# Transition to the experts laid out anew, and a 512-wide final product

## The chip, the cores and the metric

One core of one Trainium2 chip. The metric is the device time of one execution in microseconds; the time before is the median of three runs, 1478.5 (1477.45 to 1479.95). The five compute queues are PE (matrix products), ACT, DVE, POOL, and SP, which here only issues DMAs. A second row of PE in the profile, PEld, is its weight loads.

## The reference

The input x is 8 x 3072 x 256. Three parts follow one another:

```
X = rfft(x, axis=1)                                  # per batch, along the 3072 tokens
Yr = Xr @ w_r - Xi @ w_i + b_r ;  Yi = Xr @ w_i + Xi @ w_r + b_i
y = irfft(softthreshold(Yr) + 1j * softthreshold(Yi))

logits = y @ phi                                     # all 24576 tokens, 32 slots
d = softmax over tokens ; slot_in = d.T @ y          # 32 x 256
slot_out[e] = relu(slot_in[e] @ w1[e]) @ w2[e]       # 8 experts, 4 slots each, 1024 wide
z = (softmax over slots of logits) @ slot_out

h = z @ w_in                                         # 1024 wide
u = h * softmax(h) ; ln = (u - mean) / sqrt(var + 1e-6) * g_ln
out = ln @ w_out                                     # 256 wide
```

The softmax over tokens needs all batches before the first expert can start; the last part needs the experts before its first token. w_in and w_out arrive as 64-bit words and are turned into 32-bit floats on the chip.

## The kernel before

**Phase 1 (0 to about 600 us)** goes over 8 batches of 12 tiles: the Fourier transform as matrix products, the mixing weights, the inverse, the logits, and a running softmax over tokens whose weighted sums (`acc`) are formed in the spectrum (`slots`). The order is written out by hand: `after(lag, fn)` puts a step on a heap, to be issued `lag` ticks later, and the table `LAG` holds the lags. Every engine executes its own list in that order; a wait of one instruction holds up everything behind it on the same engine.

**The decoding** of w_in and w_out lies in phase 1. `decode` (L623 to L646) reads one of eight pieces (128 x 512 words of 64 bits, tile `raw`) with an SP DMA (L634), eight DVE operations, one per tile step, turn it into floats in the tiles `da`, `db`, `dm`, and `dec_out` writes `da` to `win_dram` or `wout_dram` (L660). The next piece's read is issued right behind that write.

**The transition (about 600 to 658 us).** When phase 1's memory is given back, SP issues the read of g_ln (tile `gl`) and of the decoded w_out (`wo`, 1 MB), then of the experts' weights: `wt` (15 of 512 KB), `ws` (11 of 256 KB). POOL scales `wo` by `gl` (L136). Meanwhile the last batch's softmax runs through a chain of small steps: `fwd2` (spectrum of the token weights, `dh`), `sums4` (L604) and `sums` for the running denominator, then `slots`. `gmean` forms the column mean of `wo` and subtracts it (POOL, L600). `csoft`, `csoft2`, `csoft3`, `c_x`, `c_out` make the last batch's softmax over slots and write it to `c_dram`. Behind that come 11 more `ws`, then w_in (`wi`, 1 MB), then the first read of `c_dram` (`ct`). The experts are `ph` (slots times w1), `h1` (relu: ACT L847, DVE L848), transposes, `po` (times w2), `so`; `psl` and `sot` put the slot outputs into place, and `pg` is slot outputs times w_in in four f32 products. So `gst` holds the 32 slots' rows of h, and the last part never forms z.

**Phase 2 (658 us to the end)** takes 192 tiles of 128 tokens. For each tile PE does, in this order, `hmat(i+2)` (two products 512 wide, `hps`), `trans(i)` (eight transposes of u, `pu`), and `prod(i-1)`, the product with w_out. To keep f32 accuracy with the fp32r format, u and w_out are both split into a high and a low part, `uh + ul` and `gw_h + gw_l`, and `prod` adds up three of the four products:

```
for a, w in ((uh, gw_h), (uh, gw_l), (ul, gw_h)):
    for f in range(8):
        mm(ps, a[:, f, :], w[:, f, :], n == 0, n == 23)
```

ACT copies the result (`osb`, L1027), does the exponentials (`expo`), `uh` (L971) and the squares (`vari`); DVE the row maxima (L938), u (L953) and `ul` (L979); POOL scales four tiles at once by the reciprocal standard deviation (L1032) and prepares the pieces of `c`.

Of the kernel before, what the change touches and what calls it, by code (L numbers as in the profile page):

```python
# [33 lines left out]
def kernel(  # L34
# [96 lines left out]

    def load_g():
        SP.dma_start(out=gl, in_=g_ln.rearrange("(k p) -> p k", p=128))
        SP.dma_start(out=wo, in_=wout_dram.rearrange("(k p) d -> p k d", p=128))
        for k in range(8):
            POOL.tensor_scalar(out=wo[:, k, :], in0=wo[:, k, :], scalar1=gl[:, k:k + 1], scalar2=-float(DFF) ** 1.5, op0=ALU.mult, op1=ALU.mult)  # L136


    def phase1(pl: ExitStack, pr_: ExitStack):
# [12 lines left out]
        raw_p = right("raw_p", 1)  # L152
# [339 lines left out]
        def csoft(b):  # L492
# [5 lines left out]
            after(LAG["csoft2"], csoft2, b, c)  # L498

        def csoft2(b, c):  # L500
            ACT.activation(out=c, in_=c, func=AF.Exp)
            after(LAG["csoft3"], csoft3, b, c)

        def csoft3(b, c):
# [36 lines left out]
        def dtr(b, h):  # L541
# [51 lines left out]
        def gmean(z):  # L593
            if z == 0:
                small["pg"] = psg.tile([128, D], F32, name="pgm")
            for k in range(4 * z, 4 * z + 4):
                mm(small["pg"], ones, wo[:, k, :], k == 0, k == 7)
            if z:
                ACT.activation(out=gm[:, 0, :], in_=small["pg"], func=AF.Copy, scale=1.0 / DFF)
                POOL.tensor_tensor(out=wo, in0=wo, in1=gm.to_broadcast([128, 8, D]), op=ALU.subtract)  # L600

        def sums4(b):
            s4 = sm("s4", [1, 4, 32])
            DVE.tensor_scalar(out=s4, in0=small["dh", b][0:1, 0, 0:1, :].to_broadcast([1, 4, 32]), scalar1=float(N), scalar2=None, op0=ALU.mult)  # L604
# [20 lines left out]
        def decode(src, dst):  # L625
            raw = raw_p.tile([128, 512], I64, name="raw", tag="raw")
            a = raw_p.tile([128, 512], I32, name="da", tag="da")
            c = raw_p.tile([128, 512], I32, name="db", tag="db")
            m = raw_p.tile([128, 512], I32, name="dm", tag="dm")
            v = raw.bitcast(I32).rearrange("p (n two) -> p n two", two=2)  # L630
            hi = v[:, :, 1]
            lo = raw.bitcast(U32).rearrange("p (n two) -> p n two", two=2)[:, :, 0]
# [12 lines left out]
                lambda: dec_out(dst, f),  # L645
            ])  # L646

        def dec_step():
            if not dec_ops and decs:
                decode(*decs.pop(0))  # L650
                return
            if dec_ops:
                dec_ops.pop(0)()
                if len(dec_ops) == 1:
                    dec_ops.pop(0)()
                    if decs:
                        decode(*decs.pop(0))
# [133 lines left out]
        load_ws(NS - NT)  # L791
        while heap:
# [3 lines left out]
    def phase2(p2: ExitStack, pw: ExitStack):  # L796
        k_p = p2.enter_context(tc.tile_pool(name="k2_p", bufs=1))
        c_p = p2.enter_context(tc.tile_pool(name="c_p", bufs=2))
        gw_h = k_p.tile([128, 8, D], F32R, name="gw_h")
        gw_l = k_p.tile([128, 8, D], F32R, name="gw_l")  # L800
# [33 lines left out]
        for eh in range(2):  # L834
# [14 lines left out]
            h1s[eh] = h1  # L849
        load_c(0, 1)  # L850
# [12 lines left out]
        DVE.tensor_tensor(out=gw_l, in0=wo, in1=gw_h.bitcast(F32), op=ALU.subtract)  # L863

        for eh in range(2):
# [4 lines left out]
            DVE.tensor_copy(out=so[:, eh, :], in_=po)  # L870
# [327 lines left out]
```

## Time and profile before

| | |
|---|---|
| median of three runs | 1478.5 us (1477.45 to 1479.95) |
| profiled execution | 1476.49 us, its span 1474.7 us |
| PE busy | 1422.3 us, 96% of the span |
| DVE, ACT, POOL busy | 1192.1 us (81%), 1065.2 us (72%), 671.9 us (46%) |

The span runs from the first to the last instruction that the profile holds; the execution's own time is 1.8 us longer. A busy PE is not a PE that is needed: what sets the end is read from the chain of waits, stage by stage.

### The profile page before, as it was taken

The page shows a single profiled execution, that of the slowest core. Times are in us where ns is not written, and L with a number is a line of the kernel's source. Part 1 is how long each engine was busy: PE and PEld are TensorE (multiplying, and loading weights), DVE is VectorE, ACT ScalarE, POOL GpSimd, SP SyncE. Part 2 cuts the span into 40 slices and gives each one's busy share as a digit, 9 for nine tenths or more (in the row PEclk, how much of TensorE's full clock was granted, in tenths as well). Part 3 has the DMA queues.
Part 4 walks back from the last instruction along what each step waited for, and adds up shares of the span by engine and source line. Part 5 has one row for each costly group of instructions (what it writes and reads, how often), then busy time and mean ns, then how long its engine had stood idle before and what let it go on. Part 6 is the DMA issues. An engine that isn't in the chain of part 4 may idle for free.

```text
span 1474.7 us, 31675 instructions
## 1 busy us (share of the span) xinstructions
PE 1422.3 (96%) x12300; PEld 1293.8 (88%) x12300; DVE 1192.1 (81%) x1885; ACT 1065.2 (72%) x2169; POOL 671.9 (46%) x703
## 2 busy tenths in 40 slices
PE   6999999999999999779999999999999999999999
PEld 3888887878788888539999999999999999999998
DVE  6788878887878688548888888888888888888886
ACT  5667565756565655327888888888888888888887
POOL 5556554656465633323344343443434434344343
PEclk8999999999999999898999999999999999999999
DMA  9965554546354540780111111111111111111001
GB/s 268 297 188 147 152 156 128 163 130 181 116 165 117 146 157 30 257 250 30 44 56 46 44 44 44 57 53 50 44 44 58 44 44 44 44 58 45 30 29 44
DMA packets 80102, 149.17 MB, mean 101 GB/s; under 512 B 9104, under 2 KB 45712, under 8 KB 79952
## 3 DMA queue, kind: packets, MB, share of 16 engines
q1 hardware_dynamic: 79952, 147.15, 31.8%
q8 instruction: 96, 1.57, 0.4%
q14 instruction: 54, 0.44, 0.1%
HBM read 91.55 MB, written 55.57 MB: 100 GB/s over the span
## 4 chain that ended last, share of the span: by engine, by line
PE 76%; DVE 11%; DMA 7%; issue 3%; ACT 2%; POOL 1%; SPq 0%; DVEq 0%; ACTq 0%; POOLq 0%
PE po L87 37%; PE pu L90 11%; PE hps L87 6%; PE pb L87 6%; PE s L87 3%; PE pm L87 3%; PE xps L87 3%; PE pa L87 2%; DMA xc<-in_x_dram 2%; DMA ad<-asb 2%; PE sps L90 1%; DVE yb L330 1%; DVE yb L331 1%; DVE xl L289 1%; DVE dm_sb L560 1%
## 5 line engine op out<-in xcount | busy, mean ns | idle before, releaser
L938 DVE TENSOR_REDUCE st<-hps 128x1 f32<-128x1024 f32 x192 | 235.1, 1225 | 121.4 <-PE hps L87 121.4
L979 DVE TENSOR_TENSOR ul<-pu,uh 128x512 fp32r<-128x512 f32 x384 | 246.4, 683 | 0.8 <-ACT uh L971 0.8
L953 DVE SCALAR_TENSOR_TENSOR u<-hps,e 128x1024 f32<-128x1024 f32 x192 | 233.3, 1215 | 2.2 <-ACT e L945 2.1
L334 POOL TENSOR_TENSOR s<-yb,s 128x512 f32<-128x512 f32 x95 | 132.2, 1391 | 223.5 <-DVE s L333 208.5
L87 PE MATMUL po<-gw_h,uh 128*128 128x256 f32 x1536 | 231.1, 293 | 0.0
L988 ACT ACTIVATE sq<-u,st 128x1024 f32<-128x1024 f32 x192 | 224.4, 1169 | 0.0
L945 ACT ACTIVATE e<-hps,st 128x1024 f32<-128x1024 f32 x192 | 213.2, 1110 | 2.9 <-DVE st L938 2.9
L87 PE MATMUL po<-gw_l,uh 128*128 128x256 f32 x1536 | 214.0, 282 | 0.0
L87 PE MATMUL po<-gw_h,ul 128*128 128x256 f32 x1536 | 212.8, 280 | 0.0
L971 ACT ACTIVATE uh<-pu 128x512 fp32r<-128x512 f32 x384 | 208.9, 604 | 3.0 <-PE pu L90 2.9
L90 PEld LDWEIGHTS pu<-ident,u 128*128 128x128 f32 x1536 | 180.7, 141 | 26.0 <-issue 0.4
L90 PE MATMUL pu<-ident,u 128*128 128x128 f32 x1536 | 200.6, 274 | 0.0
L87 PEld LDWEIGHTS po<-gw_h,uh 128*128 128x128 f32 x1536 | 196.5, 191 | 0.0
L87 PEld LDWEIGHTS po<-gw_l,uh 128*128 128x128 f32 x1536 | 196.2, 189 | 0.0
L87 PEld LDWEIGHTS po<-gw_h,ul 128*128 128x128 f32 x1536 | 196.2, 188 | 0.0
L226 POOL TENSOR_TENSOR x<-xc,x 96x512 fp32r<-96x512 f32 x120 | 164.8, 1381 | 41.2 <-ACT x L225 37.4
L1032 POOL TENSOR_TENSOR os<-osb,st 128x1024 f32<-128x1024 f32 x47 | 89.1, 1896 | 180.6 <-issue 172.9
L1027 ACT ACTIVATE osb<-po 128x256 f32<-128x256 f32 x188 | 72.3, 385 | 115.1 <-PE po L87 115.1
L252 ACT ACTIVATE asb<-s 96x512 f32<-96x512 f32 x112 | 66.7, 596 | 82.7 <-PE s L87 72.2
L913 POOL TENSOR_TENSOR c<-ct,c 32x512 fp32r<-32x512 f32 x96 | 123.3, 1285 | 6.7
L1008 POOL TENSOR_TENSOR st<-st 128x4 f32<-128x4 f32 (+1 forms) x51 | 10.2, 200 | 254.7 <-ACT sq L988 254.5
L87 PE MATMUL hps<-gst,c 128*128 128x512 f32 x384 | 120.5, 396 | 5.8 <-DVE u L953 4.3
(189 smaller groups left out, 2628.4 us busy)
## 6 DMA issues: line engine op xcount, KB each, us to landing
apt<-ad SPq DMA_DIRECT2D x96, 256.0 KB, 4.1
out_dram<-os SPq DMA_DIRECT2D x47, 512.0 KB, 2.6
xc<-in_x_dram SPq DMA_DIRECT2D x56, 384.0 KB, 3.9
ad<-asb SPq DMA_DIRECT2D x56, 384.0 KB, 3.5
ct<-c_dram SPq DMA_DIRECT2D x96, 128.0 KB, 2.7
wt<-in_moe_w_dram SPq DMA_DIRECT2D x21, 512.0 KB, 9.5
ws<-in_moe_w_dram SPq DMA_DIRECT2D x22, 256.0 KB, 5.7
xc<-in_x_dram SPq DMA_DIRECT2D x16, 192.0 KB, 5.1
```

The lines of the kernel that those rows point to most:

```text
L87: PE.matmul(out=out, lhsT=lhsT, rhs=rhs, start=start, stop=stop)
L90: PE.transpose(out=out, in_=in_, identity=ident[0:k, 0:k])
L226: POOL.tensor_tensor(out=lo, in0=t, in1=hi.bitcast(F32), op=ALU.subtract)
L334: (DVE if (b, t) == (B - 1, NT - 1) else POOL).tensor_tensor(out=s, in0=yb, in1=s, op=ALU.subtract)
L913: POOL.tensor_tensor(out=c4[z], in0=src[z], in1=c4[z].bitcast(F32), op=ALU.subtract)
L938: DVE.tensor_reduce(out=st[:, 0, k:k + 1], in_=hps[i], op=ALU.min, axis=AX.X)
L945: ACT.activation(out=e, in_=hps[i], func=AF.Exp, bias=st[:, 0, k:k + 1], scale=-1.0, accum_out=st[:, 1, k:k + 1])
L953: DVE.scalar_tensor_tensor(out=u, in0=hps.pop(i), scalar=1.0, in1=et.pop(i), op0=ALU.mult, op1=ALU.mult, accum_out=st[:, 2, k:k + 1])
L971: ACT.activation(out=uh[:, 4 * hf:4 * hf + 4, :], in_=ut[i, hf], func=AF.Copy)
L979: DVE.tensor_tensor(out=ul[:, 4 * hf:4 * hf + 4, :], in0=ut.pop((i, hf)), in1=uht[i][0][:, 4 * hf:4 * hf + 4, :].bitcast(F32), op=ALU.subt ...
L988: ACT.activation(out=sq, in_=ut.pop(i), func=AF.Square, bias=st[:, 2, k:k + 1], scale=-float(DFF), accum_out=st[:, 3, k:k + 1])
L1032: POOL.tensor_tensor(out=os2, in0=o, in1=q, op=ALU.mult)
```

## The change

**In the decoding**, `raw`, `da` and `db` become parts of one tile, `dec`, that shares its single buffer with `wo` and later with `wi_h` (tag `wo`, one buffer). Two pieces therefore never lie in the chip at the same time. `load_g` moves to the end of the decoding, in phase 1, and the scaling by g_ln becomes one DVE operation on `gl` and eight ACT operations, one per tile step.

**In the transition**, `gmean` is split 5 + 3 and moved ahead; the subtraction of the mean goes from POOL to DVE, at the start of phase 2's function; `sums4` goes from DVE to ACT, in every batch; the last batch's softmax steps get lags of their own. w_in is read into a tile of its own behind the first 11 `ws` and split into fp32r parts `wi_h` and `wi`; `sot` is split too, and `pg` becomes twelve fp32r products instead of four in f32. The first `ct` is read ahead of the last 11 `ws`. `gw_l` is formed between the two experts' `h1`.

**In phase 2**, `gw_h` and `gw_l` lie interleaved in one tile, so that `uh` is multiplied with both in one product of 512 columns; `ul` times `gw_h` goes into the first half of the same result. The two halves are added by POOL (one more operation for four tiles), in the last four tiles by DVE.

```diff
-    csoft_last=16, head=4, ...
+    csoft_last=5, csoft2_last=4, csoft3_last=4, c_x_last=12, head=4, ...
...
     def load_g():
+        wo = gw_t["wo"] = g_p.tile([128, 8, D], F32, name="wo", tag="wo")
         SP.dma_start(out=gl, in_=g_ln.rearrange("(k p) -> p k", p=128))
         SP.dma_start(out=wo, in_=wout_dram.rearrange("(k p) d -> p k d", p=128))
-        for k in range(8):
-            POOL.tensor_scalar(out=wo[:, k, :], in0=wo[:, k, :], scalar1=gl[:, k:k + 1], ...)
+    def scale_g(k):
+        wo = gw_t["wo"]
+        ACT.activation(out=wo[:, k, :], in_=wo[:, k, :], func=AF.Copy, scale=gl[:, k:k + 1])
...
-                POOL.tensor_tensor(out=wo, in0=wo, in1=gm.to_broadcast([128, 8, D]), op=ALU.subtract)
...
-            DVE.tensor_scalar(out=s4, in0=small["dh", b][0:1, 0, 0:1, :].to_broadcast([1, 4, 32]), scalar1=float(N), ...)
+            ACT.activation(out=s4, in_=small["dh", b][0:1, 0, 0:1, :].to_broadcast([1, 4, 32]), func=AF.Copy, scale=float(N))
...
         def decode(src, dst):
-            raw = raw_p.tile([128, 512], I64, name="raw", tag="raw")
-            a = raw_p.tile([128, 512], I32, name="da", tag="da")
-            c = raw_p.tile([128, 512], I32, name="db", tag="db")
-            m = raw_p.tile([128, 512], I32, name="dm", tag="dm")
+            z = g_p.tile([128, 2048], I32, name="dec", tag="wo")
+            raw, a, c = z[:, 0:1024].bitcast(I64), z[:, 1024:1536], z[:, 1536:2048]
+            m = g_p.tile([128, 512], I32, name="dm", tag="dm")
...
                 decode(*decs.pop(0))
+                if not decs:
+                    dec_ops.extend([load_g, lambda: None, scale_gl] + [lambda k=k: scale_g(k) for k in range(8)])
...
         load_ws(NS - NT)
+        SP.dma_start(out=wi.bitcast(F32), in_=win_dram.rearrange("(k p) f -> p k f", p=128))
...
-        wi = t_p.tile([128, 2, DFF], F32, name="wi")
+        load_c(0, 0)
         load_ws(len(ws_todo))
-        SP.dma_start(out=wi, in_=win_dram.rearrange("(k p) f -> p k f", p=128))
-        load_c(0, 0)
-
+        wo = gw_t["wo"]
+        DVE.tensor_tensor(out=wo, in0=wo, in1=gm.to_broadcast([128, 8, D]), op=ALU.subtract)
         ACT.activation(out=gw_h, in_=wo, func=AF.Copy)
...
+            if eh == 0:
+                DVE.tensor_tensor(out=gw_l, in0=wo, in1=gw_h.bitcast(F32), op=ALU.subtract)
...
+        wi_h = g_p.tile([128, 2, DFF], F32R, name="wi_h", tag="wo")
+        for dh in range(2):
+            ACT.activation(out=wi_h[:, dh], in_=wi[:, dh].bitcast(F32), func=AF.Copy)
+            DVE.tensor_tensor(out=wi[:, dh], in0=wi[:, dh].bitcast(F32), in1=wi_h[:, dh].bitcast(F32), op=ALU.subtract)
...
         for fh in range(2):
-            for dh in range(2):
-                mm(pg[fh], sot[:, dh].rearrange("p k s -> p (k s)"), wi[:, dh, 512 * fh:512 * fh + 512], dh == 0, dh == 1)
+            n = 0
+            for z, w in ((sot_h, wi_h), (sot_h, wi), (sot_l, wi_h)):
+                for dh in range(2):
+                    mm(pg[fh], z[:, dh].rearrange("p k s -> p (k s)"), w[:, dh, 512 * fh:512 * fh + 512], n == 0, n == 5)
+                    n += 1
...
-            ps = po_p.tile([128, D], F32, name="po2", tag="po2")
-            n = 0
-            for a, w in ((uh, gw_h), (uh, gw_l), (ul, gw_h)):
-                for f in range(8):
-                    mm(ps, a[:, f, :], w[:, f, :], n == 0, n == 23)
-                    n += 1
+            ps = po_p.tile([128, 2, D], F32, name="po2", tag="po2")
+            for f in range(8):
+                mm(ps, uh[:, f, :], gw[:, f], f == 0, False)
+            for f in range(8):
+                mm(ps[:, 0, :], ul[:, f, :], gw[:, f, 0, :], False, f == 7)
...
-                POOL.tensor_tensor(out=os2, in0=o, in1=q, op=ALU.mult)
+                POOL.tensor_tensor(out=os2, in0=o[:, :, 0, :], in1=o[:, :, 1, :], op=ALU.add)
+                POOL.tensor_tensor(out=os2, in0=os2, in1=q, op=ALU.mult)
```

**On SP, at the first boundary between two decoded pieces**, before (`raw` is the encoded piece, `da` the decoded one, `apt`, `ad` belong to the transform; names in brackets are semaphores):

```order
L263 DMA apt<-ad 128x512 [waits DMAHW5_49]
L660 DMA win_dram<-da 128x512 [waits DMAHW6_49,DVE_49]
L634 DMA raw<-in_moe_w_in_dram 128x512 [waits DMAHW7_49]
L263 DMA apt<-ad 128x512 [waits DMAHW3_49,DMAHW2_49,PE_49]
L263 DMA apt<-ad 128x512 [waits DMAHW1_49]
```

and the same place after, where `dec` stands for both:

```order
L271 DMA apt<-ad 128x512 [waits DMAHW5_49]
L670 DMA win_dram<-dec 128x512 [waits DMAHW6_49,DVE_49]
L641 DMA dec<-in_moe_w_in_dram 128x512 [waits DMAHW7_49,DMAHW6_49]
L271 DMA apt<-ad 128x512 [waits DMAHW3_49,DMAHW2_49,PE_49]
L271 DMA apt<-ad 128x512 [waits DMAHW1_49]
```

The order is the same; the read of the next piece has one more wait, for the landing of the write just ahead of it, and everything behind it on SP stands behind that wait. There are seven such places.

**On SP, in the transition**, before:

```order
L526 DMA c_dram<-ct_sb 96x1024
L133 DMA gl<-in_moe_g_ln_dram 128x8x1
L134 DMA wo<-wout_dram 128x8x256
L113 DMA wt<-in_moe_w_dram 128x1024 x10
L121 DMA wt<-in_moe_w_dram 128x4x256 x5
L121 DMA ws<-in_moe_w_dram 128x2x256 x11
L526 DMA c_dram<-ct_sb 96x1024
L121 DMA ws<-in_moe_w_dram 128x2x256 x11
L826 DMA wi<-win_dram 128x2x1024
L810 DMA ct<-c_dram 32x1024 x16
```

and after:

```order
L535 DMA c_dram<-ct_sb 96x1024
L113 DMA wt<-in_moe_w_dram 128x1024 x10
L121 DMA wt<-in_moe_w_dram 128x4x256 x5
L121 DMA ws<-in_moe_w_dram 128x2x256 x11
L802 DMA wi<-win_dram 128x2x1024
L535 DMA c_dram<-ct_sb 96x1024
L822 DMA ct<-c_dram 32x1024 x4
L121 DMA ws<-in_moe_w_dram 128x2x256 x11
L822 DMA ct<-c_dram 32x1024 x12
```

`gl` and `wo` are gone from here, `wi` stands ahead of the last write of `c_dram`, and that write and the first four `ct` stand ahead of the last 11 `ws`.

**On PE, one tile of phase 2**, before:

```order
L87 MATMUL hps<-gst_8754,c_9072 128x512
L87 MATMUL hps<-gst_8755,c_9072 128x512
L90 MATMUL pu<-ident,u 128x128 x8
L87 MATMUL po_9409<-gw_h,uh 128x256 x8
L87 MATMUL po_9409<-gw_l,uh 128x256 x8
L87 MATMUL po_9409<-gw_h,ul 128x256 x8
```

and after:

```order
L87 MATMUL hps<-gst_8738,c_9071 128x512
L87 MATMUL hps<-gst_8739,c_9071 128x512
L90 MATMUL pu<-ident,u 128x128 x8
L87 MATMUL po_9317<-gw,uh 128x512 x8
L87 MATMUL po_9317<-gw,ul 128x256 x8
```

Sixteen products of 256 columns become eight of 512; the rest of the tile stands as it did.

## Rows read from the trace of the kernel before

**Rows 1.** The page, part 4: shares of the chain that ended last.

```profile
PE 76%; DVE 11%; DMA 7%; issue 3%; ACT 2%; POOL 1%; SPq 0%; DVEq 0%; ACTq 0%; POOLq 0%
```

**Rows 2.** Busy time by stage: PE, PEld, DVE, ACT, POOL, granted clock, DMA, GB/s.

```profile
60.00:600.00 540.00, 522.06 (x5069) 452.58 (x5071) 442.00 (x823) 327.18 (x733) 292.15 (x213) 0.99 0.48 143
600.00:658.00 58.00, 43.67 (x479) 24.92 (x467) 24.59 (x38) 14.68 (x26) 16.97 (x18) 0.88 0.96 313
658.00:1474.70 816.70, 808.77 (x6528) 781.79 (x6528) 684.58 (x960) 689.23 (x1344) 330.52 (x442) 0.99 0.13 46
```

**Rows 3.** Chain of waits, one tile of phase 2: start us, us, what.

```profile
1452.28 0.46 PE hps L87 x2
1452.74 0.87 PE pu L90 x8
1453.61 2.85 PE po L87 x24
```

**Rows 4.** Timeline of one tile: idle time ahead, and its releaser, in brackets.

```profile
686.16 0.39 ACT L1027 ACTIVATE osb<-po 128x256 f32<-128x256 f32 x1 [0.60 <-PE po L87]
...
686.62 1.23 DVE L938 TENSOR_REDUCE st<-hps 128x1 f32<-128x1024 f32 x1 [0.62 <-PE hps L87]
```

**Rows 5.** Groups by form, ACT, 700:1400: count, busy us, mean ns, idle.

```profile
L971 ACT ACTIVATE uh<-pu 128x512 fp32r<-128x512 f32 x336 | 182.5, 604 | 0.0
L1027 ACT ACTIVATE osb<-po 128x256 f32<-128x256 f32 x167 | 64.2, 385 | 100.7 <-PE po L87 100.7
```

**Rows 6.** Groups of the same stretch: POOL's scaling of four output tiles.

```profile
L1032 POOL TENSOR_TENSOR os<-osb,st 128x1024 f32<-128x1024 f32 x42 | 79.6, 1896 | 161.4 <-issue 157.5 <-ACT osb L1027 3.8
```

**Rows 7.** Timeline of SP's queue at the first decode boundary.

```profile
98.03 0.32 SPq L660 DMA_DIRECT2D win_dram<-da  x1
98.40 0.43 SPq L634 DMA_DIRECT2D raw<-in_moe_w_in_dram  x1
```

**Rows 8.** Tile da: landing time of the decoded piece's write, all eight.

```profile
DMA to landing us min/median/max: 2.2/2.5/3.3
```

**Rows 9.** Tile raw: landing time of the encoded piece's read, all eight.

```profile
DMA to landing us min/median/max: 4.3/5.2/7.2
```

**Rows 10.** DMA issues 130:141: KB each, median us to landing.

```profile
xc<-in_x_dram SPq DMA_DIRECT2D x2, 384.0 KB, 3.7
```

**Rows 11.** Chain of waits, 60:600: pieces just behind decode boundaries.

```profile
99.85 5.96 DMA ad<-asb
...
296.94 5.71 DMA raw<-in_moe_w_out_dram
...
399.30 5.53 DMA ad<-asb
```

**Rows 12.** Chain of waits across the transition.

```profile
620.54 2.37 DVE s L604
...
636.99 4.74 DMA ws<-in_moe_w_dram
...
641.80 9.32 DMA wi<-win_dram
...
651.26 5.38 PE pg L87 x8
```

**Rows 13.** Timeline of the transition, ACT, DVE and POOL.

```profile
618.31 4.52 POOL L600 TENSOR_TENSOR wo<-wo,gm 128x2048 f32<-128x2048 f32 x1 [6.83 <-ACT gm L599]
...
622.83 0.19 DVE L613 TENSOR_SCALAR srun<-srun,mexp 128x1 f32<-128x1 f32 x1
...
638.05 1.09 ACT L847 ACTIVATE h<-ph 128x512 f32<-128x512 f32 x2 [6.55 <-DMA c_dram<-ct_sb]
...
641.88 2.28 DVE L863 TENSOR_TENSOR gw_l<-wo,gw_h 128x2048 fp32r<-128x2048 f32 x1
```

**Rows 14.** Busy time around the last product of the transition.

```profile
651.00:655.00 4.00, 3.74 (x5) 1.65 (x6) 0.00 (x0) 0.40 (x1) 1.87 (x2) 0.59 0.84 241
```

**Rows 15.** Timeline of the last output tile.

```profile
1471.35 0.47 ACT L1024 ACTIVATE osb<-po,st 128x256 f32<-128x256 f32 x1 [2.37 <-PE po L87]
```

More of the change, by code (lines that the diff above doesn't have):

```diff
@@ L550, in dtr @@
                 if b == B - 1:
-                    after(LAG["d_x"] + 2, gmean, 1)
+                    gmean(5, 8)
                 after(LAG["d_x"], d_x, b, 0)
@@ L590, in slots, with gmean @@
                 DVE.scalar_tensor_tensor(out=acc, in0=ps[:, 0:D], scalar=mexp[:, 1:2], in1=acc, op0=ALU.mult, op1=ALU.add)
[L593 to L594 removed]
+        def gmean(k0, k1):
+            if k0 == 0:
                 small["pg"] = psg.tile([128, D], F32, name="pgm")
[L596 to L598 removed]
+            for k in range(k0, k1):
+                mm(small["pg"], ones, gw_t["wo"][:, k, :], k == 0, k == 7)
+            if k1 == 8:
                 ACT.activation(out=gm[:, 0, :], in_=small["pg"], func=AF.Copy, scale=1.0 / DFF)
[L600 removed]
         def sums4(b):
             s4 = sm("s4", [1, 4, 32])
[L604 removed]
+            ACT.activation(out=s4, in_=small["dh", b][0:1, 0, 0:1, :].to_broadcast([1, 4, 32]), func=AF.Copy, scale=float(N))
             after(LAG["sums"], sums, b, s4)
@@ L653, in dec_step @@
                 dec_ops.pop(0)()
-                if len(dec_ops) == 1:
+                if dec_ops and getattr(dec_ops[0], "is_out", False):
                     dec_ops.pop(0)()
-                    if decs:
-                        decode(*decs.pop(0))
+                    dec_step()
         def dec_out(dst, f):
@@ L798, in phase2 @@
         c_p = p2.enter_context(tc.tile_pool(name="c_p", bufs=2))
-        gw_h = k_p.tile([128, 8, D], F32R, name="gw_h")
-        gw_l = k_p.tile([128, 8, D], F32R, name="gw_l")
+        gw = k_p.tile([128, 8, 2, D], F32R, name="gw")
+        gw_h, gw_l = gw[:, :, 0, :], gw[:, :, 1, :]
         gst = [k_p.tile([128, 512], F32R, name=f"gst{fh}") for fh in range(2)]
@@ L869, in phase2 @@
                     mm(po[32 * cg:32 * cg + 32, :], h1ts[eh][:, k, 32 * cg:32 * cg + 32], w2t[4 * eh + cg, k], k == 0, k == 7)
-            DVE.tensor_copy(out=so[:, eh, :], in_=po)
+            DVE.tensor_scalar(out=so[:, eh, :], in0=po, scalar1=-1.0, scalar2=None, op0=ALU.mult)
         psl = pt.tile([128, 2, 32], F32, name="psl", tag="pt")
@@ L1018, in outp @@
             if k == 0:
-                osb[0] = o_p.tile([128, 4, D], F32, name="osb", tag="osb")
+                osb[0] = o_p.tile([128, 4, 2, D], F32, name="osb", tag="osb")
             o = osb[0]
@@ L1023, in outp @@
                 rstd(j, slice(k, k + 1))
-                ACT.activation(out=o[:, k, :], in_=pot.pop(i), func=AF.Copy, scale=stt[j][:, 4, k:k + 1])
-                SP.dma_start(out=v[:, k, :], in_=o[:, k, :])
+                ACT.activation(out=o[:, k], in_=pot.pop(i), func=AF.Copy, scale=stt[j][:, 4, k:k + 1])
+                DVE.tensor_tensor(out=o[:, k, 0, :], in0=o[:, k, 0, :], in1=o[:, k, 1, :], op=ALU.add)
+                SP.dma_start(out=v[:, k, :], in_=o[:, k, 0, :])
                 return
-            ACT.activation(out=o[:, k, :], in_=pot.pop(i), func=AF.Copy)
+            ACT.activation(out=o[:, k], in_=pot.pop(i), func=AF.Copy)
             if k == 3:
```

45 lines of the change are left out of this document (25 added, 20 removed).

## The prediction

> **What bounds the kernel now.** I read the page first for its chain of waits: PE carries 76% of the chain, DVE 11% and DMA 7% [rows 1], so neither "PE-bound" nor "DMA-bound" holds everywhere, and the change touches three stages with different limits. The table by stage shows which [rows 2]. From 658 us on PE is busy 808.77 of 816.70 us at a clock of 0.99 (of 2.4 GHz) while the DMA engines stand at 0.13: phase 2 is PE's. From 60 to 600 us PE is busy 522 of 540 and DMA 0.48. From 600 to 658 us PE has 43.67 of 58 and DMA 0.96: the transition waits for transfers.
>
> In phase 2 the chain goes from one PE group to the next without a gap: 0.46 us for two `hps`, 0.87 for eight transposes, 2.85 for 24 products [rows 3], together 4.18 us a tile, and 192 x 4.18 = 803 of the 817 us. The others wait: ACT 0.60 us a tile, DVE 0.62 [rows 4]. A microsecond of phase 2 is therefore a microsecond of PE. The chain of phase 1 shows, behind the places where one decoded piece follows another, DMAs that somebody waits for [rows 11]: three of the seven are shown, three more look alike. So SP's order is not free there, though PE looks busy.
>
> **The final product.** 24 products cost 2.85 us, or 119 ns for 256 columns; the two `hps`, which are 512 columns wide and in the same format, cost 0.46, or 230 ns each [rows 3]. New tile: 0.46 + 0.87 + 8 x 0.230 + 8 x 0.119 = 4.12, against 4.18: -0.06 us a tile, **-11.5 us** over 192. The trace shows no train of eight 512-wide products, so this is bounded: 0 if a wide product costs two narrow ones, and -15.4 if the 0.46 is really 0.455 (7.7 at 0.465). I take the middle, since the format, the width and the engine are those of the row. A narrow product is only 3% dearer than half a wide one; nothing here halves.
>
> What could take the place of PE: ACT's `osb` becomes 512 wide like `uh`, 604 ns in place of 385 [rows 5], +0.22 us, so its 0.60 us of waiting becomes 0.60 - 0.22 - 0.06 = 0.32; DVE keeps 0.56. POOL has one more operation of 1.9 us for four tiles, and waits 161 us for 42 such groups, 3.8 us each [rows 6]. It fits, with about half to spare. So PE remains the bound, and the gain stands. In the last tile `osb` and the add lie behind PE [rows 15]: 0.22 for the width, about 0.4 for an add of 128x256 (an estimate from ACT's 385 ns for that size [rows 5]) and a hand-over: **+0.75**.
>
> **The decoding.** Before, the read of the next piece is issued 0.37 us behind the write of the last [rows 7] and lands 5.2 us later (median) [rows 9], so it is there 5.57 us after the write was issued; the write shares the engines with it. With one tile for both, the read is issued when the write has landed. That is 2.2 us if it has the engines to itself (the smallest of 2.2, 2.5, 3.3) [rows 8]. Then the read has the engines alone: the row for an input tile of 384 KB, almost alone in its stretch, says 3.7 us [rows 10]; `raw` has 512 KB, and 128 KB more at 313 GB/s [rows 2] is 0.4, so 4.1. Together 2.2 + 0.05 + 4.1 = 6.35, or 0.78 later than before. What is queued behind it on SP (`apt`, `ad`, `xc`) is late by the same, as it shares the engines with the read in both versions. PE and DVE wait for those three just there [rows 11], so nothing covers it: 7 x 0.78 = 5.5. `load_g` is an eighth place, since `wo` takes the same buffer and waits for the last write: **+6.2** for eight.
>
> The bounds: 0.3 a place if the engines work the two in parallel so well that only the issue is late; and 2.2 + 0.05 - 0.37 = 1.9, up to 2.9 with a landing of 3.3, if the whole wait passes on to `apt`, `ad` and `xc`. That is 2.4 to 23 us for eight. I take 0.78, since in the old order the time of the write is mostly in the 5.2 us already.
>
> **The transition.** Gains. (1) `wo` and `gl` go out of the stretch in which DMA is the limit: 1 MB at 313 GB/s [rows 2] is 3.3 us. (2) `sums4`, a 1x128 operation, took 2.37 us [rows 12] and ended when POOL's 4.52 us subtraction of the mean ended [rows 13]; the operation behind it took 0.19. The subtraction leaves POOL, and `sums4` leaves DVE: about -1.5 with ACT's own start. (3) `wi` lands ahead of the last `ws`, so `pg` no longer waits for it (9.32 us in the chain [rows 12]) but for `po`, and with it for the last `ws`.
>
> Here a rule of the Trainium skill bears on the row. On the page "SBUF — State Buffer", section "Who interferes with whom", it says that DVE in its two-port modes and GpSimd lock each other out for a whole instruction, and that the order of issue decides who blocks. By that rule the 2.37 us were a lock, and the trace agrees as far as the same end goes; by the same rule the subtraction on DVE, with both inputs in SBUF, could now lie behind a POOL operation. By it the gain is 1.5; without it, if `sums4` was late for another reason, 0.
>
> Costs. `h1` waited for `c_dram`'s write to land (6.55 us of ACT's idle time [rows 13]), and that write stands now behind `wi`, 1 MB: +3.3 on it, which takes back (1). The last 11 `ws` come behind that write and behind `ct`, so they come no earlier by (1) than by it. On DVE the subtraction of the mean (2 to 4.5 us) comes ahead of the first `h1`, and `gw_l`, 2.28 us [rows 13], ahead of the second. Against this, `pg` was 5.38 us [rows 12], and part of it at half clock (0.59 from 651 to 655 [rows 14], after a pause of PE); twelve wide products are 12 x 0.23 = 2.8 at full clock, 5.5 at half. The split of `wi` is four operations, each half the size of `gw_l`'s, so about 1.1 us each by an estimate from its 2.28; two lie on ACT and two on DVE, beside the 64 products of `po`; without that cover they cost 2.3. The eight scalings of `wo` on ACT lie in phase 1, where ACT has 213 of 540 us free [rows 2]: nothing. I count **-1**: the bytes are the same but for `wo`, the end of the stream is 3.3 earlier, and about two of that go to the chain from the last `ws` through `po`, `so`, `psl` to `pg`. Bounds: -6 (all of (1) and 2.6 of `pg`), +3 (`h1` and `ws` late by a landing).
>
> **The sum.** -11.5 + 0.75 + 6.2 - 1 = -5.55 on the profiled execution's 1476.49: 1470.9. The profiled execution lay 2.0 us below the median of the runs, so on the median: 1478.5 - 5.55 = about 1473.
>
> **The rivals.**
> *The transition gives all it could*: -6 in place of -1, so 1468. For it: DMA at 0.96 and the half clock of `pg`. Against: each early transfer pushes another one back.
> *The wide product saves next to nothing.* The width is then not the price: a product costs its columns, and only a start of a few ns is saved. Midway between the rows' 11.5 us and none, phase 2 gives 5.7, and the time is 1478.7; with none it is 1484.5. For it: 230 ns is only 8 ns off twice 119, and `hps` stands in pairs, not in trains. Against: the `hps` row is measured. The Trainium skill, "TensorE: Matmul & The Clock Gate", section "Back-to-back issue gap", gives for one product N/2.4 + about 2.5 ns, from which the saving would be just these 2.5 ns, 8 x 2.5 x 192 = 3.8 us in all, and the time 1480.6. By that rule the 119 and 230 ns of the trace should be 109 and 216, so it does not agree in size.
> *The landing wait passes on in full.* SP stands still from each write to its landing, and `apt`, `ad`, `xc` start so much later; at 2.1 us in seven places and 3.6 for `wo`, 1 MB in the midst of the transform, it is 18.5 in place of 6.2: 1485. It decides from about 1.5 us a place, where the gain of phase 2 is eaten up. For it: the waits just behind the boundaries [rows 11]. Against: the read was slowed by the write before.
> *ACT or the loop through it takes over in phase 2*, the tile stays at 4.18 us: 11.5 less, 1484.5. Against it: 0.32 us of waiting are left.
>
> **How the numbers follow.** Forecast 0.55, with a range of its own from 1468 to 1478; transition 0.16; no saving of the wide product 0.14; landing wait 0.12; ACT 0.03. A measurement of this kernel tells about 0.2% (3 us) from no change, so "same" is 1475.5 to 1481.5. The first two are faster, but 0.05 of the forecast falls into same: faster 0.66; same 0.05 + 0.14 = 0.19; slower 0.15. The range leaves out the lowest end of the transition's case and most of the two slower ones: 1463 to 1483.
>
> **What would show it.** In the profile after: the PE chain of a tile at 4.12 us, with about 1.84 for eight wide products, and ACT waiting some 0.3 us before `osb`. At each decode boundary the read's issue 2.2 to 2.5 us behind the write's; phase 1 some 6 us longer, with the longer waits on `ad`, `apt`, `xc`. The stretch from the first `wt` to the first `hps` about 1 us shorter, `pg` behind `po` and not behind `wi`. I am wrong if a tile stays at 4.18, if phase 1 grows by over 12 us or not at all, or if `h1` waits so long that the transition gets longer.

## The result, and the profile after

The changed kernel takes 1490.8 us (median of five runs, 1486.15 to 1492.98) against 1478.3 before: 1.0077 times as long, 95% interval 1.0055 to 1.0098. It was forecast to be faster. The profiled execution took 1486.99 us, its span 1485.2; it is one of two of the five at a mean granted clock of 0.984, and the other three, at 0.979 to 0.980, took 1490.8 to 1493.0, so the median lost some us more than the profile shows.

The page's chain of waits, part 4 of the profile after, looks almost like the one before [rows 1]:

```profile
PE 75%; DMA 8%; DVE 8%; issue 3%; ACT 2%; SPq 2%; POOL 1%; DVEq 0%; ACTq 0%; POOLq 0%
```

The only entry that grew by more than one point is SPq, from 0 to 2%: time in which SP's queue itself was on the path. To see where the time is, cut the run at three places that both kernels have: the last batch's logits (`pm<-st,phi_sb`), the first `hps`, and the last `hps`. The timeline of PE before:

```profile
599.63 1.07 PE L87 MATMUL pm<-st,phi_sb 128*32 128x256 f32 x16 [0.49 <-DVE srun L614]
...
658.13 1.16 PE L87 MATMUL hps<-gst,c 128*128 128x512 f32 x4 [1.51 <-DVE gst L885]
...
1456.30 0.62 PE L87 MATMUL hps<-gst,c 128*128 128x512 f32 x2
```

and after:

```profile
613.29 1.61 PE L87 MATMUL pm<-st,phi_sb 128*32 128x256 f32 x16 [0.83 <-DVE srun L622]
...
674.47 1.16 PE L87 MATMUL hps<-gst,c 128*128 128x512 f32 x4 [1.51 <-DVE gst L907]
...
1461.46 0.62 PE L87 MATMUL hps<-gst,c 128*128 128x512 f32 x2
```

The differences of these rows give four stages, with the span's end as the last cut:

| us | phase 1 | transition | tiles | end | span |
|---|---|---|---|---|---|
| before | 599.6 | 58.5 | 798.2 | 18.4 | 1474.7 |
| after | 613.3 | 61.2 | 787.0 | 23.7 | 1485.2 |
| difference | +13.7 | +2.7 | -11.2 | +5.3 | +10.5 |
| forecast | +6.2 | -1 | -11.5 | +0.75 | -5.55 |

**The tiles** do in kind what was forecast. The chain after, one tile (start us, us, what), answers to [rows 3]:

```profile
1445.07 0.46 PE hps L87 x2
1445.53 0.87 PE pu L90 x8
1446.40 2.81 PE po L87 x16
```

2.81 us in place of 2.85. From 687.28 us on (673.38 before) one tile's `hps` follows the other after 4.140 us on the mean in place of 4.187 (774.18 and 782.92 us for 187 steps): 8.7 us less. The other 2.4 of the 11.2 us lie in the one step before that. Its window (busy time of PE, PEld, DVE, ACT, POOL, then clock, DMA share, GB/s), before:

```profile
666.53:673.38 6.85, 6.85 (x34) 6.55 (x35) 4.62 (x7) 4.34 (x8) 3.17 (x3) 0.59 0.01 2
```

and after:

```profile
682.88:687.28 4.40, 4.40 (x26) 3.62 (x27) 4.40 (x7) 4.11 (x8) 3.21 (x3) 1.00 0.02 6
```

PE was busy throughout, before at 0.59 of its clock and after at 1.00. In e1, with the wide product, this step took 6.93 us, so the 2.4 us are not the wide product's.

ACT's groups by form (700:1400) answer to [rows 5]; `osb` has grown to 598 ns and still waits, 58.8 us for 170:

```profile
L993 ACT ACTIVATE uh<-pu 128x512 fp32r<-128x512 f32 x338 | 183.3, 602 | 0.0
L1050 ACT ACTIVATE osb<-po 128x512 f32<-128x512 f32 x170 | 101.6, 598 | 58.8 <-PE po L87 58.8
```

**Phase 1.** SP's queue at the first boundary after, answering to [rows 7]:

```profile
100.20 0.32 SPq L670 DMA_DIRECT2D win_dram<-dec  x1
102.21 0.33 SPq L641 DMA_DIRECT2D dec<-in_moe_w_in_dram  x1
102.65 0.85 SPq L271 DMA_DIRECT2D apt<-ad  x2
```

The read is issued 2.01 us behind the write, where it was 0.37, and `apt` behind it. The DMA groups of the stretch 95:460 (KB each, median us to landing) answer to [rows 8, 9]:

```profile
dec<-in_moe_w_out_dram SPq DMA_DIRECT2D x4, 512.0 KB, 4.2
dec<-in_moe_w_in_dram SPq DMA_DIRECT2D x3, 512.0 KB, 4.6
win_dram<-dec SPq DMA_DIRECT2D x4, 256.0 KB, 2.0
wout_dram<-dec SPq DMA_DIRECT2D x4, 256.0 KB, 2.5
```

For comparison the same view before: 

```profile
raw<-in_moe_w_out_dram SPq DMA_DIRECT2D x4, 512.0 KB, 5.0
raw<-in_moe_w_in_dram SPq DMA_DIRECT2D x3, 512.0 KB, 5.4
```

From the write's issue to the read's landing it is now 2.0 + 4.6 = 6.6 us for w_in and 2.5 + 4.2 = 6.7 for w_out; before, 0.4 + 5.4 = 5.8 and 0.4 + 5.0 = 5.4. By these medians a boundary is later by 0.8 us in four places (the read of w_out's first piece, behind w_in's last write, among them) and by 1.3 in three: 7.1 for the seven. The stretch from the issue of the first write to that of the last shows it directly (columns as above), before:

```profile
98.03:446.77 348.74, 335.46 (x3219) 289.13 (x3221) 284.90 (x521) 216.89 (x485) 204.07 (x149) 0.99 0.52 153
```

after, and in e3 (an experiment below, whose phase 1 is that of the changed kernel):

```profile
100.20:456.81 356.61, 335.25 (x3221) 288.85 (x3223) 283.05 (x517) 217.12 (x489) 204.04 (x149) 0.99 0.51 150
```

```profile
99.86:462.46 362.60, 341.23 (x3223) 294.18 (x3225) 283.35 (x517) 217.42 (x489) 204.20 (x149) 0.97 0.50 147
```

The stretch is 7.9 us longer after, and PE is busy in it for the same 335 us at the same clock of 0.99: all 7.9 are idle time. In e3 another 6 us come on top, and there PE is busy 6 us longer, at 0.97 of its clock. Behind the last boundary `load_g` follows. SP's queue there:

```profile
456.81 0.38 SPq L670 DMA_DIRECT2D wout_dram<-dec  x1
457.24 0.47 SPq L137 DMA_DIRECT2D gl<-in_moe_g_ln_dram  x1
460.80 0.36 SPq L138 DMA_DIRECT2D wo<-wout_dram  x1
461.26 0.51 SPq L216 DMA_DIRECT2D xc<-in_x_dram  x1
461.88 2.08 SPq L271 DMA_DIRECT2D apt<-ad  x4
```

SP stands 3.1 us (from 457.7 to 460.8), and then 1 MB goes ahead of `xc` and `apt`. From the last write to the logits' cut it takes 156.5 us in place of 152.9. The remaining 2.2 of the 13.7 us are there ahead of the first boundary.

**The transition.** SP's queue:

```profile
642.80 0.37 SPq L802 DMA_DIRECT2D wi<-win_dram  x1
643.59 0.33 SPq L535 DMA_DIRECT2D c_dram<-ct_sb  x1
651.51 1.72 SPq L822 DMA_DIRECT2D ct<-c_dram  x4
653.27 5.63 SPq L121 DMA_DIRECT2D ws<-in_moe_w_dram  x11
```

and the chain of waits beside it:

```profile
643.59 7.77 DMA c_dram<-ct_sb
...
658.38 8.61 DMA ws<-in_moe_w_dram
...
669.93 3.05 PE pg L87 x12
```

The read of `ct` waits for the write of `c_dram`, whose bytes stand behind `wi` and the first `ws` and take 7.77 us to land. For 7.6 us SP issues nothing, and the last 11 `ws` come that much later; `po` waits for them, and `pg` for `po`. `pg` itself went from 5.38 [rows 12] to 3.05 us, as hoped.

**The end.** The timeline behind the last `hps`:

```profile
1462.34 2.40 POOL L1055 TENSOR_TENSOR os<-osb 128x1024 f32<-128x1024 f32 x1 [3.70 <-ACT osb L1050]
...
1464.81 1.89 POOL L1056 TENSOR_TENSOR os<-os,st 128x1024 f32<-128x1024 f32 x1
...
1467.97 0.58 POOL L1031 TENSOR_TENSOR st<-st,mhalf 128x1 f32<-128x1 f32 x1
...
1468.58 0.69 ACT L1046 ACTIVATE osb<-po,st 128x512 f32<-128x512 f32 x1 [3.12 <-POOL st L1031]
1469.16 1.11 ACT L967 ACTIVATE e<-hps,st 128x1024 f32<-128x1024 f32 x1
```

In the last four tiles `osb` is scaled by ACT, with a factor that POOL has to make first. POOL is busy with the two large operations of the group before until 1466.70, and only then does the five small ones. ACT stands 3.12 us at `osb`, and the exponentials of the next tile stand behind it in ACT's order; so `u`, the transposes and PE are late in turn. Before, with one large operation on POOL, the same `osb` waited 0.71 us for it:

```profile
1460.80 0.47 ACT L1024 ACTIVATE osb<-po,st 128x256 f32<-128x256 f32 x1 [0.71 <-POOL st L1009]
```

Behind its wait of 2.83 us PE then ran at a lower clock (0.90 over the whole end). Eight products 512 wide, after, and at the same place in e1, where the wait was 2.86 us and the clock over the end 0.96:

```profile
1473.30 3.30 PE L87 MATMUL po<-gw,uh 128*128 128x512 f32 x8
```

```profile
1461.54 2.11 PE L87 MATMUL po<-gw,uh 128*128 128x512 f32 x8
```

The end of e1, which has the same code there, is 3.4 us longer than before and not 5.3. So about 1.9 of the 5.3 go with the clock; the rest is the wait for POOL and what the wider `osb` and the add cost.

### The profile page after: what moved, and what is told of

The parts are those of the page before. It is cut to its first block, busy times and chain, and to the rows that moved or that the text cites. A ratio compares the mean times of both kernels' runs of the same rounds, so it can differ in the third digit from the quotient of the medians.

```text
span 1485.2 us, 28653 instructions
## 1 busy us (share of the span) xinstructions
PE 1418.7 (96%) x10768; PEld 1219.8 (82%) x10768; DVE 1210.7 (82%) x1885; ACT 1111.5 (75%) x2188; POOL 778.6 (52%) x741
## 4 chain that ended last, share of the span: by engine, by line
PE 75%; DMA 8%; DVE 8%; issue 3%; ACT 2%; SPq 2%; POOL 1%; DVEq 0%; ACTq 0%; POOLq 0%
PE po L87 36%; PE pu L90 11%; PE pb L87 7%; PE hps L87 6%; PE s L87 4%; PE pm L87 3%; PE xps L87 3%; PE pa L87 3%; DMA xc<-in_x_dram 2%; PE sps L90 2%; DMA apt<-ad 1%; DMA ad<-asb 1%; DMA ws<-in_moe_w_dram 1%; SPq L121 1%; DVE xl L297 1%
## 5 line engine op out<-in xcount | busy, mean ns | idle before, releaser
L87 PE MATMUL po<-gw,uh 128*128 128x512 f32 x1536 | 407.6, 407 | 0.0
L87 PEld LDWEIGHTS po<-gw,uh 128*128 128x128 f32 x1536 | 275.7, 189 | 52.5
L87 PEld LDWEIGHTS po<-gw,ul 128*128 128x128 f32 x1536 | 207.9, 188 | 17.8
L87 PE MATMUL po<-gw,ul 128*128 128x256 f32 x1536 | 210.8, 279 | 0.0
L1055 POOL TENSOR_TENSOR os<-osb 128x1024 f32<-128x1024 f32 x47 | 113.1, 2406 | 173.5 <-ACT osb L1050 173.5
L1050 ACT ACTIVATE osb<-po 128x512 f32<-128x512 f32 x188 | 112.3, 598 | 65.1 <-PE po L87 65.1
L87 PE MATMUL s<-x,df_h 96*96 96x512 f32 x240 | 105.9, 443 | 19.0 <-ACT asb L260 9.8
L87 PEld LDWEIGHTS xps<-d_sb,apt 128*128 128x128 f32 x768 | 99.2, 194 | 17.8 <-DMA apt<-ad 5.6
L87 PE MATMUL xps<-d_sb,apt 128*128 128x128 f32 x768 | 106.3, 282 | 4.0 <-DMA apt<-ad 3.9
```

Of the source, the lines that this page charges most:

```text
L87: PE.matmul(out=out, lhsT=lhsT, rhs=rhs, start=start, stop=stop)
L1055: POOL.tensor_tensor(out=os2, in0=o[:, :, 0, :], in1=o[:, :, 1, :], op=ALU.add)
```

## The experiments

All are timed beside runs of the kernel before on the same chip; its medians there were 1475.8 to 1476.7, and its runs went from 1471.5 to 1483. Ratios are to those. One profiled execution gives the stages, and these spread too: the transition of before's own instructions (before, e1, e5, b_wide_tail) came out as 58.5 to 60.7, once as 65.3 with PE at a lower clock (0.75 over its first 30 us). So a difference of 2 us in that stage alone is no finding.

| us | phase 1 | transition | tiles | end | ratio (95%) |
|---|---|---|---|---|---|
| e1_wide_only | 599.4 | 60.7 | 789.5 | 21.8 | 0.9970 (0.9955 to 0.9985) |
| e2_dec_once | 602.4 | 60.2 | 789.5 | 22.2 | 0.9995 (0.9980 to 1.0009) |
| e3_ct_behind_ws | 616.9 | 55.1 | 788.6 | 23.7 | 1.0067 (1.0045 to 1.0089) |
| e4_tail | 617.1 | 61.7 | 789.5 | 19.1 | 1.0067 (1.0049 to 1.0086) |
| e5_wait_only | 608.9 | 58.7 | 797.9 | 18.4 | 1.0073 (1.0052 to 1.0095) |
| e6_sums4_act | 598.9 | 56.2 | 797.5 | 18.4 | 0.9982 (0.9966 to 0.9999) |
| g_all | 602.8 | 56.9 | 789.0 | 19.1 | 0.9941 (0.9925 to 0.9957) |
| g_wi_behind_c | 600.6 | 56.8 | 787.5 | 19.1 | 0.9927 (0.9909 to 0.9944) |
| b_wide_tail | 600.9 | 65.3 | 787.5 | 19.1 | 0.9942 (0.9922 to 0.9962) |
| b_wide_tail_sums4 | 596.7 | 57.2 | 789.4 | 19.1 | 0.9927 (0.9905 to 0.9949) |

**e1_wide_only**: the kernel before with the phase 2 part of the diff alone (its last three hunks and the tile `gw`).

> The kernel before with nothing of the change but the 512-wide product in phase 2 (interleaved weights, 512-wide osb, POOL's extra operation, DVE's add in the last four tiles). Theory (gain and loss of phase 2 are its own): the tiles take 4.14 us in place of 4.19, -11.2 us between the first and the last hps, and the end behind the last hps is 5.3 us longer because POOL's two scaling operations (2.4 and 1.9 us) hold up the small operations that the last four tiles' osb waits for; together about -6, so 1472.4. Rival (the gain of the tiles needs the rest of the change, or the longer end comes from PE's clock and not from POOL): no change, 1478, or with the end as before 1467.

1473.4 us, ratio 0.9970: 4.4 us less by the ratio, 3.2 between the medians, where about 6 were expected. The tiles got 8.7 us shorter, the end 3.4 longer, without anything of the decoding or the transition. So the gain and its own tax are phase 2's. The end was longer by less than the 5.3 that were named: `osb` waits for POOL as long as in the changed kernel (3.15 us), but PE's clock stays up behind it. So a share of the changed kernel's end, 1.9 us, goes with the clock, as the rival had it.

**e2_dec_once**:

```diff
-            z = g_p.tile([128, 2048], I32, name="dec", tag="wo")
+            if "z" not in dec_t:
+                dec_t["z"] = g_p.tile([128, 2048], I32, name="dec", tag="wo")
+            z = dec_t["z"]
```

> The changed kernel with one edit: the tile dec is taken from its pool once and used for all eight pieces, so that the read of the next piece (it goes into another part of the tile than the write reads) no longer waits for the landing of the write. Memory and all else as in the changed kernel. Theory (the landing wait at seven boundaries costs 7.9 us): about 8 less than the changed kernel, 1483 where that has 1491; the shift that stays by 455 us is 2 or less, and the jump at load_g stays 3. Rival (phase 1 is longer for another reason: sums4 on ACT, the eight scalings, other places in memory): no more than 2 less.

1476.4 us, ratio 0.9995: as long as before, and 14 us less than the changed kernel, where 8 were expected. Phase 1 is 10.9 us shorter: 8.4 between the first write and the last, 0.9 ahead of the first, and 1.6 behind the last, where the jump at `load_g` was expected to stay at 3 us and came to 1.6. SP's queue at the first boundary:

```profile
99.33 0.32 SPq L673 DMA_DIRECT2D win_dram<-dec  x1
99.70 0.43 SPq L644 DMA_DIRECT2D dec<-in_moe_w_in_dram  x1
```

0.37 us again, in the same memory: only whether the tile is taken anew differs. DVE's wait for a piece, over all boundaries, was 6.2 us in 6 before, here 5.7 in 6, and in the changed kernel 12.2 in 7.

**e5_wait_only**: the kernel before with the one merged tile alone.

```diff
-            raw = raw_p.tile([128, 512], I64, name="raw", tag="raw")
-            a = raw_p.tile([128, 512], I32, name="da", tag="da")
-            c = raw_p.tile([128, 512], I32, name="db", tag="db")
+            z = raw_p.tile([128, 2048], I32, name="dec", tag="dec")
+            raw, a, c = z[:, 0:1024].bitcast(I64), z[:, 1024:1536], z[:, 1536:2048]
```

> The kernel before with one part of the change alone: raw, da and db become one tile that is taken anew for each piece, so that each read of a piece waits for the landing of the write before it (seven places). Nothing else differs. Theory (the loss of phase 1 is this wait and the PE pauses, with a lower clock, that it makes): phase 1 gets 9 to 13 us longer, 1487 where the kernel before has 1476.6; the DVE yb operations shift by about 1 to 2 us at each of the seven boundaries. Rival (the loss needs the other edits of phase 1 too, the eight scalings on ACT or sums4): under 5 us.

1487.3 us, ratio 1.0073; phase 1 is 9.3 us longer, nothing else moves. With e2 this closes the question for the seven boundaries: taking the wait away takes 8.4 us away between the first write and the last, and putting it in alone brings 8.0 there (356.7 us in place of 348.7), as much as the changed kernel lost there. About 1.2 us of the 9.3 are there before the first boundary (the first `yb` operations), as in most of these executions. What the changed kernel lost behind the last boundary is not in e5, which has no `load_g` in phase 1.

**e3_ct_behind_ws**:

```diff
-        load_c(0, 0)
         load_ws(len(ws_todo))
+        load_c(0, 0)
```

> The changed kernel with the first reads of c_dram put back behind the last 11 ws; w_in stays early. Theory (SP stands still at those reads until c_dram's write has landed, 644 to 651 us, and the last 11 ws are late by it): ws is issued from about 644 on, po no longer waits for it, h1 still waits for c_dram's write; the first hps comes about 6 us earlier, 1485 where the changed kernel has 1491. Rival (the stream of bytes sets the end, not the issue): 0 to 1 us less.

1486.8 us, where 1485 was expected. The transition takes 55.1 us in place of 61.2, the 6 that were expected. SP's queue:

```profile
645.84 0.33 SPq L535 DMA_DIRECT2D c_dram<-ct_sb  x1
646.51 10.29 SPq L121 DMA_DIRECT2D ws<-in_moe_w_dram  x11
```

The time alone does not show it: 1.0067 and the changed kernel's 1.0077 overlap. The profiled phase 1 of e3 was 616.9 us against 613.3 in the changed kernel's own profile, at a mean clock of 0.979 against 0.984; the changed kernel's runs have both clocks, with times from 1486 to 1493. That stage's spread is of the size of what is looked for.

**e4_tail**: the last eight tiles are scaled by ACT; POOL's small operations for a tile are issued behind its `vari`, two tiles ahead; DVE's add comes behind `ulo`.

```diff
+        def fin(i):                       # called behind vari(i)
+            j, k = divmod(i, 4)
+            if NG - 2 <= j < NG:
+                rstd(j, slice(k, k + 1))
+            while late_add:
+                o, k, v = late_add.pop(0)
+                DVE.tensor_tensor(out=o[:, k, 0, :], in0=o[:, k, 0, :], in1=o[:, k, 1, :], op=ALU.add)
+                SP.dma_start(out=v[:, k, :], in_=o[:, k, 0, :])
```

> The changed kernel with the end written anew: the last eight tiles (in place of four) are scaled by ACT and added by DVE, and POOL's five small operations for each are issued two tiles ahead, so that POOL has no large operation there. Theory (POOL's two large operations held up osb, and by it the exponentials behind it on ACT): the time from the last hps to the end is 18 to 18.7 us in place of 23.7, so 5 less, 1486 where the changed kernel has 1491. Rival (the end is longer because a product of 512 columns costs more at PE's lower clock): no more than 1 less.

1488.1 us, where 1486 was expected. The end is 19.1 us in place of 23.7 (18 to 18.7 was expected), and 19.1 again in all four later kernels with this edit. `osb` of the tile where it waited 3.12 us for POOL now waits 0.26 for PE:

```profile
1472.56 0.69 ACT L1044 ACTIVATE osb<-po,st 128x512 f32<-128x512 f32 x1 [0.26 <-PE po L87]
```

A wait for POOL is left at the second of the eight tiles, 1.17 us, and one step between two `hps` takes 4.5 us there in place of 4.14. PE's clock over the end is 0.99: with the wait its lower clock went too. PE's wait and its clock thus left together, so e4 does not tell their shares. As with e3, the whole time (1.0067) doesn't separate 4.6 us from phase 1's spread; the stage does.

**e6_sums4_act**: the kernel before with `sums4` on ACT.

> The kernel before with sums4 on ACT in place of DVE, and nothing else. Theory (the 2.37 us on DVE were a wait for POOL's subtraction): in the transition the 1x128 operation takes about 0.3 us and the slots product starts 1.5 to 2 us earlier; what follows waits for transfers, so the first hps comes 0 to 1.5 us earlier: 1476. Rival (the operation was late for another reason): the same start of the slots product.

1474.2 us, ratio 0.9982, with an interval that just leaves out 1. The timeline:

```profile
617.59 4.54 POOL L600 TENSOR_TENSOR wo<-wo,gm 128x2048 f32<-128x2048 f32 x1 [7.28 <-ACT gm L599]
...
620.34 0.29 ACT L604 ACTIVATE s<-dh_sb 1x128 f32<-1x128 f32 x1
...
620.99 2.80 PE L87 MATMUL pm<-s,dh_sb 128*32 128x256 f32 x48
```

POOL does the same 4.5 us, ACT does the 1x128 operation in 0.29 in its midst where DVE took 2.37 [rows 12], and the slots product takes 2.80 us. That DVE was held by POOL's operation and by nothing of its own is seen in before too: of its eight `sums4` on DVE the last, the one beside POOL's 4.52 us, took 2.35 us, and the seven others 0.15 to 0.21 (ns, min/median/max):

```profile
L604 DVE TENSOR_SCALAR s<-dh_sb x8: 150/208/2355, 164.9 to 620.5; 1x128 f32<-1x128 f32 x8
```

The slots product before:

```profile
623.64 4.48 PE L87 MATMUL pm<-s,dh_sb 128*32 128x256 f32 x48 [0.31 <-DVE srun L614]
```

It took 4.48 us in e1 and e5 too, and 5.35 in b_wide_tail. In all four PE had waited 2.3 us just ahead of it, and was granted 0.62 to 0.63 of its clock in it, in b_wide_tail 0.50; in e6, after a wait of 0.77 us, it was 1.00. So the pause went with a second loss, in clock. How much of that reaches the first `hps` one profile cannot tell.

**g_all**: e2, e3 and e4 together, with `load_g` four tile steps later.

> The changed kernel with four edits: the decoding's tile taken once, load_g four tile steps later, the first reads of c_dram behind the last 11 ws, and the end of the last eight tiles as in e4. Theory (the four losses add up and lie in different places): phase 1 at most 1.5 us longer than before, the transition 55 us as in e3, the tiles 787 to 789.5, the end 19: 1464 to 1466 where the kernel before has 1476.6. Rival (they cover each other, an earlier stage only waits at the next): 1470 or more.

1468.7 us, ratio 0.9941: 8 us less than before, and 8 less than e2, clear of both intervals. The end and the tiles are as expected, the transition 1.8 longer than expected, and phase 1 3.1 longer than before (2.4 of it are there by 82 us, ahead of the first boundary, and nothing is added where `load_g` now stands). So the losses add up, though not to the 12 us that were expected; the time lies between the 1464 to 1466 of the theory and the rival's 1470, nearer to the rival.

**g_wi_behind_c**: as g_all, with `wi` behind `c_dram`'s write and ahead of the last 11 `ws`.

> The same with the read of w_in put behind the last write of c_dram and ahead of the last 11 ws. Theory (h1 waits for the landing of that write, which stands behind 1 MB of w_in): the write lands 2 to 3 us earlier, h1 starts so much earlier, and the first hps comes 1 to 3 us earlier than in g_all. Rival (w_in is then late for its split, and the split holds up what is behind it on ACT and DVE): the same or up to 3 us later.

1466.3 us, ratio 0.9927. `h1` waits 2.61 us for that write in place of 5.00, as the timelines of g_wi_behind_c and of g_all show:

```profile
637.20 1.08 ACT L861 ACTIVATE h<-ph 128x512 f32<-128x512 f32 x2 [2.61 <-DMA c_dram<-ct_sb]
```

```profile
639.71 1.09 ACT L861 ACTIVATE h<-ph 128x512 f32<-128x512 f32 x2 [5.00 <-DMA c_dram<-ct_sb]
```

but the transition is the same, 56.8 and 56.9: `po` then waits for the last `ws`. The wait moved. The 3.8 us between the two profiles lie in phase 1 (2.2) and the tiles (1.5), where nothing was edited, and the intervals overlap. No gain is shown.

**b_wide_tail** (the kernel before with the wide product and e4's end) and **b_wide_tail_sums4** (the same, `sums4` on ACT):

> The kernel before with the 512-wide product and the end of the last eight tiles as in e4; decoding, g_ln's scaling and the transition as before. Theory (the gain of the change lies in phase 2 alone): tiles 787 to 790, end 19.1, the rest as before, so 10 less than before: 1467 where that has 1476.7, and within 3 of g_wi_behind_c. Rival (the transition laid out anew is worth something once its waits are gone): 5 or more slower than g_wi_behind_c.

> The same with sums4 on ACT as well. Theory (POOL's subtraction of the mean held it up on DVE): 1.5 to 2.5 less than b_wide_tail, 1465, and the fastest of the kernels. Rival (the 2.3 us that e6 showed in the transition are the spread between executions): the same as b_wide_tail.

1468.5 and 1465.9 us, ratios 0.9942 and 0.9927. The first, with the decoding and the transition of before, is as fast as g_all; the second as fast as g_wi_behind_c, with a few lines edited. So nothing of the new layout of the transition is shown to be worth anything here, once its waits are mended, and no loss by it is shown either. (The profiled execution of b_wide_tail, with its transition of 65.3 us, was the slowest of seven, 1474.6 us.) Between the two, 2.6 us agree with e6, but the intervals overlap. The fastest time, 0.7% under before, is had in both ways.

## Why the prediction was wrong

The forecast was 5.55 us less, and the profile has 10.5 more. Of the 16 us between them phase 1 has 7.5, the end 4.6, the transition 3.7 and the tiles 0.3. Two of the signs of being wrong that the prediction names came true: phase 1 grew by over 12 us, and the transition got longer.

**The wide product: right in kind, its number with some luck.** 11.5 us forecast, 11.2 measured in the profile (8.7 to 10.7 in the other kernels with the wide product), but only 8.7 of them are the wide product's; 2.4 come from PE's clock in one step of the profile before. Eight wide products cost 1.86 us and not 1.84, which is the 0.465 a pair for which the prediction named 7.7. The price of the `hps` row so nearly held for a train of eight, and ACT and DVE still wait for PE (0.35 and 0.45 us a tile). The rival on ACT falls; the rival on the saving was half right, as 8.7 lies midway between the 11.5 and its 5.7.

**The decoding: the mechanism was right, the term too small.** It was priced at 5.5 us for seven boundaries and 0.78 for `load_g`. The write lands as estimated (2.0 to 2.5 against 2.2); the read, thought to have the engines alone, took 4.2 to 4.6 and not 4.1, with `apt` issued 0.44 us behind it. The seven cost 7.9 us in the profile after and 8.0 in e5, 1.1 a place, all of it idle time of PE. In e3 and e4, with the same phase 1, the stretch is 13.9 and 12.6 longer than before, and PE is 4 to 6 us longer busy in it at a clock of 0.97 and 0.98. The sum had no term for that.

For `load_g` the price of a small boundary was the wrong row: SP stood 3.1 us and then put 1 MB ahead of the transform's reads. In the changed kernel the `yb` operations shift by 3.2 us between 411 and 482 us, in e2 by 1.6, and in g_all and g_wi_behind_c, with `load_g` later, by nothing. Of the 3.6 us behind the last write 1.8 are longer busy time of PE, whose clock was 0.96 over the 38 us behind that write. The 2.2 us ahead of the first boundary are no loss of the change's: e1, with the code of before, has 4.4 there. The rival with the wait passed on in full had the right sign; it was held at 0.12. Its 2.1 a place was too much for the seven, its 3.6 for `wo` near the 3.2.

**The transition: the step that failed in kind.** The forecast had `ct` ahead of the last `ws`, and saw that `c_dram`'s write would land behind 1 MB. It priced that as a delay of a transfer, +3.3 against -3.3, and said that the last `ws` "come no earlier". It did not ask what SP itself does at `ct`: it waits for that write, with everything behind it unissued, for 7.6 us. The DMA share of the transition fell from 0.96 [rows 2] to 0.89 (from 615 to 674 us). -1 became +2.7, and e3 takes 6 us of it back by two lines changed about, to 55.1 us, which is 3.4 below before; g_all has 56.9. So the forecast's small gain was there, behind a wait that had no price.

**The end: missed.** +0.75 was forecast for the width and the add. e4, which takes the wait for POOL away, comes to 19.1 - 18.4 = 0.7, though with the adds at another place than the changed kernel has them. What was missed is 4.6 us: the wait for POOL, about 2.7, and PE's lower clock behind it, about 1.9 by the difference to e1. "It fits, with about half to spare" was read from POOL's mean idle time over the stage [rows 6], while the last four tiles need POOL's result within one tile's time, at the moment when the doubled operation runs. The prediction looked at the last of these tiles [rows 15], which waits for PE, and not at the first, which waited for POOL already before.

**sums4: right on the operation, not resolved in the stage.** The operation is freed (e6: 2.37 to 0.29), and the slots product behind it is shorter by 1.7. The stage of e6 is 2.3 us shorter than before's, which is of the size of its spread. The section "Who interferes with whom" of the Trainium skill's page "SBUF — State Buffer" says that DVE in its two-port modes and GpSimd lock each other out for a whole instruction; the trace agrees, as DVE's operation ends with POOL's and ACT's is not held up, though no run here shows which mode DVE was in. Such a lock shows at another operation too. In the changed kernel a 128x2 operation on DVE ends with POOL's `c_sb`, after 1.20 us (before, it took 0.71 and ended with POOL's `c_sb` too):

```profile
637.89 1.91 POOL L517 TENSOR_TENSOR c_sb<-c_sb,rs 96x1024 f32<-96x1024 f32 x1 [6.76 <-DVE srun L621]
638.67 1.20 DVE L626 TENSOR_SCALAR mexp<-mexp,srun 128x2 f32<-128x2 f32 x1
```

The subtraction of the mean, for which the prediction feared the lock, took 2.27 us on DVE with no POOL operation beside it.

**What stays open**: why the same phase 1 comes out as 613 us in one execution (after) and 617 in two others (e3, e4). The rows show the lower clock that goes with it, not what starts it. And why g_all gained 8 us and not 12.

## What to carry to other kernels

Where tiles share a buffer, ask for each DMA that fills it whose landing it now waits for, and what else stands in that queue: a wait of 2 to 3 us on SP's queue, at seven places, cost 8 us, nearly what the shape of a product gained over all tiles. Price a wait by what cannot be issued behind it, not by the bytes alone; and check an engine's spare time at the place where its result is needed within a deadline (the last tiles above all), not as a mean over the stage. When parts of one memory are reused, keeping one tile and writing to its parts let the next read start beside the last write (e2), at no cost in memory.

## What the runs showed of the hardware

A PE pause of 2.3 us ahead of the 48 slots products went with a lower clock in them: 4.48 us at 0.62 to 0.63 (before, e1, e5) and 5.35 at 0.50, the lower level of 1.2 GHz (b_wide_tail), where they took 2.80 at 1.00 with a pause of 0.77 (e6). Short waits can so cost twice, but they did not each time: behind a pause of 2.83 us in the end of the changed kernel eight wide products took 3.30 us, behind one of 2.86 in that of e1 2.11.

A product of 512 columns in a train of eight, in fp32r at full clock, costs nearly what it costs in a pair: 2.81 - 0.95 = 1.86 us for eight, or 233 ns, against 230.
